# Folding the column transforms of a spectral block over f and -f: fewer products on TensorE, more sums on GpSimd and VectorE

## The chip, the core and the metric

The kernel runs on one core of a Trainium2 chip. The metric is the device time of one execution in microseconds (us). The engines are named as in the profile: PE (TensorE, matrix products; PEld is its weight loads), DVE (VectorE), ACT (ScalarE), POOL (GpSimd) and SP (SyncE, which here only issues DMAs). Each engine works through its own queue in order; queues wait for each other by semaphores.

## What is computed

The reference, cut to what matters (one batch, S = 2048 rows, D = 512 columns, F = 1376, all in float32):

```python
def _A_ref(x, w_r, w_i):                      # spectral filter
    X = rfft2(x, axes=(-2, -1))
    X = X * (w_r + 1j * w_i)
    return irfft2(X, s=(S, D), axes=(-2, -1))

def _B_ref(x, w1, b1, w2):                    # Dense -> Mish -> Dense
    h = x @ w1 + b1
    return (h * tanh(softplus(h))) @ w2

mod = (silu(c) @ w_mod).reshape(1, 6, 1, -1)
sa, ca, ga, sb, cb, gb = (mod[:, i] for i in range(6))
h = layernorm(x) * (1 + ca) + sa
x = x + ga * _A_ref(h, A_w_r, A_w_i)
h = layernorm(x) * (1 + cb) + sb
x = x + gb * _B_ref(h, B_w1, B_b1, B_w2)
```

## The kernel before

The transforms are products with constant matrices. The 2048 rows are seen as 128 x 16 (16 blocks n), the 512 columns as 128 x 4, and the half spectrum as 64 column frequencies q with 8 values each (4 lanes, real and imaginary). The order of each engine's instructions is that of the program, stage by stage, written by hand; tile pools with two buffers per tag ("g1", "g2", "t", "y", "h") and two PSUM banks per tag ("A" to "D") decide how far one step can run ahead of another.

**Stage one**, for each block n (the loop at L342): `p1_row` multiplies the transposed x by row constants that hold the scale 1 + ca (four full-precision products, L203). DVE takes the statistics of x (`norm_sums`, L117 and L118), ACT guesses the reciprocal deviation (`norm_guess`), DVE refines it (`norm_refine`, L130). `p1_mean` (L218) subtracts the mean's part, `p1_cast` and `p1_low` (L234, L241) split the result into a high and a low half in the reduced-precision type. `p1_split` does the same for the column constants of the block (ACT L195, POOL L196) and makes a negated copy (L197). `p1_col` then forms the complex column product with nine reduced-precision products (L248 to L250), and `p1_save` copies it to `a_sb`. The gate's and shift's sums that this stage needs are the `shift_sum` calls; `shift_rows` ends the stage.

**Stage two** works on 17 groups of column frequencies: fifteen of four, one of three, and one that holds the special frequencies (`z_...`). `seq` is their order, with the special group fifth. For each group: `p2_in` transposes `a_sb` on PE and copies it to a buffer z (ACT, L464), POOL adds the shift to one column per frequency (`p2_shift`, L472); `p2_mul` applies the 16-point part of the row transform (L482); `p2_prod` multiplies by the filter on DVE (L498) and adds and subtracts (L503, L504: both on POOL, the first on DVE for the first three and last two groups); `p2_back` transposes (L515) and copies (L518); `p2_out` applies the inverse (L528); `store_d` writes the result to `d` with two copies and two negated copies on ACT. The first eight `p2_in` come ahead of the loop (LEAD = 8); in step s of the loop stand `p2_prod` of group s, `p2_mul` of s + 1, `p2_in` of s + 3 (from s = 5), `mod_late`, `p2_back` of s - 2 and `p2_out` of s - 3. `mod_late` forms the gates and second shift and scale from `w_mod`, sixteen sums on DVE over the steps (L98, L100, L110); `mod_fetch` loads what they need.

**Stage three**, for each block n (the loop at L902): `p3_col` makes the inverse column transform with eight products (four with the constants `kc[0]`, L663, and four with `kc[1]`, L664), ACT copies, `p3_row` makes the inverse row transform (four products, L673) and DVE adds it to x (L676). Between them stand the second statistics (L117), the loads and splits of w1 (ACT L621, POOL L622) and w2 (L714, L715), and the first blocks' normalisation and transposition (L655).

**The MLP** runs 48 items with a lag of two items between its first and second product (`mlp`, L858).

## Time and profile before

| | |
|---|---|
| median of 3 runs | 392.95 us (391.5 to 393.79) |
| the profiled execution | 391.52 us, of which the span is 389.4 us |
| granted PE clock, mean | 1.0 |
| instructions | 7386 |
| stage one: first save to last save of the column product | about 16.3 to 50.1 us |
| stage two: first transposes to last store | about 50.2 to 98.9 us |
| stage three: first inverse product to first product of the MLP | 98.9 to 142.1 us |
| MLP | 142.1 to 389.4 us |

How to read the profile's lines: a group's line names the source line, the engine, the operation, output and inputs, the shape and the count; behind the bar stand its busy time in us and the mean of one in ns, then the idle time of the engine just ahead of it and what ended that. A line of the order of time starts with the start and the duration in us. One full-precision product is two MATMUL records; a reduced-precision one and a transposition are one record each. A matmul's end is modelled, so the distance between starts is what counts.

### The profile page before, as it was taken

How to read it: one execution, taken by the hardware profiler on the slowest of the kernel's cores; microseconds unless marked ns; L12 is line 12 of the kernel's file. 1: busy time of each engine (PE TensorE's matmuls, PEld its weight loads, DVE VectorE, ACT ScalarE, POOL GpSimd, SP SyncE). 2: the span in 40 equal slices, each digit the busy share in tenths (PEclk: the TensorE clock that was granted, in tenths of full speed). 3: DMA queues.
4: the chain of work that ended last, by engine and by line, in shares of the span. 5: the costliest groups of instructions: out<-in, count | busy, mean ns of one | idle time of the engine just before them, and what ended most of it. 6: DMA issues, size and time to landing. Idle time of an engine off the chain costs nothing.

```text
span 389.4 us, 7386 instructions
## 1 busy us (share of the span) xinstructions
PE 383.1 (98%) x2752; PEld 355.4 (91%) x2752; DVE 298.8 (77%) x668; ACT 247.9 (64%) x546; POOL 96.1 (25%) x132
## 2 busy tenths in 40 slices
PE   8999999999999999999999999999999999999996
PEld 8889889999999998999998998999999999899984
DVE  2888978876299989887856965965966875987993
ACT  1798756678559648975855765674674674594751
POOL 0687737665077533300000000000000010017000
PEclk9999999999999999999999999999999999999999
DMA  7999993472132411100100100100100200123011
GB/s 237 383 323 339 347 344 109 133 300 63 47 124 78 145 49 28 56 3 0 56 0 3 54 2 0 56 0 2 55 2 0 76 0 2 46 65 106 3 54 54
DMA packets 21027, 36.44 MB, mean 94 GB/s; under 512 B 3680, under 2 KB 6592, under 8 KB 20736
## 3 DMA queue, kind: packets, MB, share of 16 engines
q1 hardware_dynamic: 20992, 35.98, 27.1%
q8 instruction: 21, 0.34, 0.3%
q14 instruction: 14, 0.11, 0.1%
HBM read 31.78 MB, written 4.19 MB: 92 GB/s over the span
## 4 chain that ended last, share of the span: by engine, by line
PE 86%; DMA 4%; DVE 3%; ACT 3%; issue 1%; SPq 1%; POOL 1%; POOLq 0%; DVEq 0%
PE bank L805 24%; PE bank L752 20%; PE bank L754 10%; PE bank L482 3%; PE bank L528 3%; PE bank L673 3%; PE bank L663 3%; PE bank L664 3%; PE bank L797 2%; PE bank L248 2%; DMA x<-in_A_x_dram 2%; PE bank L203 2%; PE bank L817 2%; PE bank L642 2%; PE bank L461 2%; DMA mraw<-in_km_dram 2%
## 5 line engine op out<-in xcount | busy, mean ns | idle before, releaser
L762 ACT ACTIVATE buf<-bank,b1n 128x256 f32<-128x256 f32 (+1 forms) x88 | 40.8, 472 | 66.8 <-PE bank L754 66.4
L763 DVE TENSOR_TENSOR buf<-buf,bank 128x256 f32<-128x256 f32 (+1 forms) x88 | 35.4, 417 | 38.6 <-ACT buf L762 38.6
L715 DVE TENSOR_TENSOR al<-buf,ah 128x512 fp32r<-128x512 f32 (+2 forms) x85 | 53.5, 653 | 0.7 <-ACT ah L714 0.7
L734 POOL TENSOR_TENSOR buf<-buf,modr 128x512 f32<-128x512 f32 (+1 forms) x3 | 3.9, 1292 | 183.0 <-DMA buf<-in_B_w_dram 175.7
L752 PE MATMUL bank<-h2e,w1h 128*128 128x512 f32 (+1 forms) x176 | 48.4, 397 | 0.0
L752 PE MATMUL bank<-h2o,w1h 128*128 128x512 f32 (+1 forms) x176 | 48.3, 396 | 0.0
L714 ACT CAST ah<-buf 128x512 fp32r<-128x512 f32 (+2 forms) x85 | 43.0, 548 | 1.2 <-DVE buf L779 1.2
L779 DVE TENSOR_TENSOR buf<-buf 128x128 f32<-128x128 f32 x148 | 39.9, 311 | 3.5 <-ACT buf L769 2.2
L769 ACT ACTIVATE buf<-buf 128x512 f32<-128x512 f32 (+1 forms) x48 | 28.6, 596 | 14.8 <-DVE buf L763 14.7
L805 PE MATMUL bank<-w2a,ah 128*128 128x256 f32 x161 | 34.9, 286 | 0.0
L752 PEld LDWEIGHTS bank<-h2o,w1h 128*128 128x128 f32 (+1 forms) x176 | 30.2, 187 | 4.5
L752 PEld LDWEIGHTS bank<-h2e,w1h 128*128 128x128 f32 (+1 forms) x176 | 30.1, 187 | 4.5
L805 PE MATMUL bank<-w2b,ah 128*128 128x256 f32 x147 | 31.8, 283 | 0.0
L754 PEld LDWEIGHTS bank<-h2o,w1l 128*128 128x128 f32 (+1 forms) x176 | 26.7, 185 | 4.2
L754 PEld LDWEIGHTS bank<-h2e,w1l 128*128 128x128 f32 (+1 forms) x176 | 26.7, 185 | 4.2
L754 PE MATMUL bank<-h2e,w1l 128*128 128x256 f32 (+1 forms) x176 | 27.8, 280 | 0.0
L754 PE MATMUL bank<-h2o,w1l 128*128 128x256 f32 (+1 forms) x176 | 27.8, 280 | 0.0
L805 PEld LDWEIGHTS bank<-w2a,ah 128*128 128x128 f32 x161 | 26.7, 191 | 0.0
L663 PE MATMUL bank<-kc,d 128*128 128x128 f32 x128 | 24.7, 275 | 0.0
L664 PE MATMUL bank<-kc,d 128*128 128x128 f32 x128 | 24.7, 275 | 0.0
L805 PEld LDWEIGHTS bank<-w2b,ah 128*128 128x128 f32 x147 | 24.6, 191 | 0.0
L117 DVE BATCH_NORM_STATS2 st<-x 128x6 f32<-128x512 f32 x32 | 22.1, 689 | 0.8 <-DMA x<-in_A_x_dram 0.4
(227 smaller groups left out, 1002.7 us busy)
## 6 DMA issues: line engine op xcount, KB each, us to landing
buf<-in_B_w_dram SPq DMA_DIRECT2D x20, 256.0 KB, 2.8
x<-in_A_x_dram SPq DMA_DIRECT2D x16, 256.0 KB, 4.9
xring<-in_x_t_dram SPq DMA_DIRECT2D x16, 256.0 KB, 5.1
wm<-in_w_mod_dram SPq DMA_DIRECT2D x16, 256.0 KB, 4.2
out_dram<-x SPq DMA_DIRECT2D x7, 512.0 KB, 2.6
mraw<-in_km_dram SPq DMA_DIRECT2D x16, 128.0 KB, 5.0
wqa<-in_w_q_dram SPq DMA_DIRECT2D x8, 256.0 KB, 4.8
wqb<-in_w_q_dram SPq DMA_DIRECT2D x8, 256.0 KB, 5.5
```

The source lines that it names most:

```text
L117: nc.vector.bn_stats(t, x[:, n, :])
L663: nc.tensor.matmul(o, dj[:, 0:128], kc[0][:, n, :], start=True, stop=False)
L664: nc.tensor.matmul(o, dj[:, 64:192], kc[1][:, n, :], start=False, stop=True)
L714: nc.scalar.copy(h, r)
L715: nc.vector.tensor_tensor(l, r, plain(h), op=ALU.subtract)
L752: nc.tensor.matmul(ps, w1h[:, k, fs], h[:, k], start=(k == 0), stop=False)
L754: nc.tensor.matmul(ps[:, 0:256], w1l[:, k, fs], h[:, k, 0], start=False, stop=(k == 3))
L762: nc.scalar.activation(o, ps[:, 256:], AF.Identity, bias=b1n[:rows, f:f + 1])
L763: nc.vector.tensor_tensor(o, o, ps[:, 0:256], op=ALU.add)
L769: nc.scalar.activation(o, o, AF.Mish)
L779: nc.vector.tensor_tensor(o, p, q, op=op)
L805: nc.tensor.matmul(o, a[p][:, e], w2[t][q][:, r], start=(own and half == 0 and t == 1 and i == 0), stop=(end and i == 2 and (n, half) != ( ...
```

## The change

The column transform is folded over the frequencies f and -f. The constants of the first column product now are 128 real columns: cosines for 64 frequencies, sines for 63, and the alternating column of frequency 64; so one real full-precision product per block (`p1_col`) takes the place of nine reduced-precision ones, and splitting, casting and the low halves go. `p1_save` turns the sine half by -i with three ACT instructions. The mean's part is made apart: POOL forms row sums times mean (`p1_rank`), and DVE scales and adds in one instruction (`p1_norm`); the first two blocks keep `p1_mean` and are scaled on ACT. `first_scale` makes the negated mean times reciprocal deviation as well (`norm_shift`).

In stage two, f and -f are joined by a sum and a difference per group, on POOL for all groups (`fold(nc.gpsimd, ...)` in `p2_in`), and taken apart again with a sum and a difference on DVE from PSUM (`fold(nc.vector, ...)` in `p2_back`); the ACT copy of `p2_back` becomes half as wide. Groups now have 127 rows. Frequency 64 of all column groups is gathered by small POOL copies in `zh` and taken through a branch of its own (`half_mul`, `half_prod`, `half_back`, `half_out`) in the last steps; its result is put in the last row of `dd` by a DMA on SP's queue. `store_d` has three ACT instructions instead of four. The sums of `mod_late` are on DVE as before.

In stage three `p3_col` needs four products instead of eight, and `kc` and `km` are half as large. The loads of `km` bring two blocks each. The w2 buffers move to other tags.

The diff, cut to its core:

```diff
     def first_scale(lo, hi):
-        norm_refine(lo, hi, -1, st.pop(("r", lo)))
+        norm_refine(lo, hi, -1 if lo < 2 else 1, st.pop(("r", lo)))
+        if lo >= 2:
+            norm_shift(lo, hi)
...
     def load_m(n):
-        nc.sync.dma_start(mraw[:, n, :], km_d[:, n, :])
+        if n % 2 == 0:
+            nc.sync.dma_start(m[:, n:n + 2, :], km_d[:, n:n + 2, :])
...
+    def p1_scale(n):
+        st["g", n] = g = buf("g1")
+        nc.scalar.activation(g, st.pop(("pg", n)), AF.Copy, scale=rstd[:, n:n + 1])
+
+    def p1_rank(n):
+        st["km", n] = t = buf("g2")
+        nc.gpsimd.tensor_scalar(t, kb, nmr[:, n:n + 1], 0.0, op0=ALU.mult, op1=ALU.add)
+
+    def p1_norm(n):
+        st["g", n] = g = buf("g1")
+        nc.vector.scalar_tensor_tensor(g, st.pop(("pg", n)), rstd[:, n:n + 1], st.pop(("km", n)),
+                                       op0=ALU.mult, op1=ALU.add)
+
+    def p1_col(n):
+        st["pa", n] = pa = bank("C")
+        nc.tensor.matmul(pa, m[:, n, :], st.pop(("g", n)), start=True, stop=True)
 
     def p1_save(n):
-        nc.scalar.copy(a_sb[:, :, n, :], st.pop(("pa", n)).rearrange("p (e q) -> p q e", e=8))
+        pa = st.pop(("pa", n)).rearrange("p (e q) -> p q e", e=8)
+        nc.scalar.copy(a_sb[0:H, :, n, :], pa[0:H])
+        nc.scalar.copy(a_sb[H:P, :, n, 0:4], pa[H:P, :, 4:8])
+        nc.scalar.mul(a_sb[H:P, :, n, 4:8], pa[H:P, :, 0:4], -1.0)
...
+            p1_col(n)
+            if n % 2 and n + 2 < N2:
+                first_scale(n + 1, n + 3)
+                p1_rank(n + 1)
+                p1_rank(n + 2)
             if n + 3 < N2:
-                p1_split(n + 3)
                 norm_sums(n + 3)
                 if n % 2 == 0:
                     first_guess(n + 2, n + 4)
+            if 1 <= n and n + 1 < N2:
+                p1_norm(n + 1)
...
+        nc.scalar.copy(dd[0:H, :, :, qs], src[0:H])
+        nc.scalar.mul(dd[H:end, :, 0, qs], src[H:end, :, 1, :], -1.0)
+        nc.scalar.copy(dd[H:end, :, 1, qs], src[H:end, :, 0, :])
...
+    def fold(eng, z, far):
+        eng.tensor_tensor(z[..., H:U], z[..., 1:H], far, op=ALU.subtract)
+        eng.tensor_tensor(z[..., 1:H], z[..., 1:H], far, op=ALU.add)
 
     def z_in():
...
+        nc.gpsimd.memset(z[:, 0:3 * P], 0.0)
...
     def z_back():
...
+        nc.gpsimd.memset(t1[:, 0:3 * P], 0.0)
         nc.gpsimd.memset(t2[0:96, 0:P], 0.0)
...
+    def half_prod():
+        pb = st.pop(("pb", "h"))[0:NQ, 0:P].rearrange("p (c j) -> p c j", c=2)
...
+    def half_out():
+        pd = bank("D")
+        nc.tensor.matmul(pd[:, 0:NQ], kv[:, 512:640], st.pop(("t", "h"))[:, 0:NQ], start=True, stop=True)
+        nc.scalar.copy(zh, pd[:, 0:NQ])
+        nc.sync.dma_start(dd[U:P].rearrange("p a c q -> p (a c) q")[:, :, 1:NQ], zh[:, 1:NQ])
 
     def p2_in(g):
...
-        nc.scalar.copy(z[:, 0:w], ps[:, 0:w])
-        st["z", g] = z
+        st["z", g] = zbuf(g)
+        z = turned(g)
+        src = ps[:, 0:nq * P].rearrange("p (q b s) -> p q b s", q=nq, b=2)
+        nc.scalar.copy(z.rearrange("p q (b s) -> p q b s", s=H)[:, :, 0:3:2, :], src)
+        fold(nc.gpsimd, z, z[:, :, P:P + U - H])
+        nc.gpsimd.tensor_copy(zh[:, q0:q0 + nq], z[:, :, 191])
...
     def p2_back(g):
...
         t = buf("t")
-        nc.scalar.copy(t[:, 0:w], pc[:, 0:w])
+        tv, src = (v[:, 0:w].rearrange("p (q s) -> p q s", s=P) for v in (t, pc))
+        nc.scalar.copy(tv[:, :, 0:H], src[:, :, 0:H])
+        fold(nc.vector, tv, src[:, :, H:U])
...
+            for i, fn in enumerate((half_mul, half_prod, half_back, half_out)):
+                if s == len(seq) - 3 + i:
+                    fn()
...
     def p3_col(n):
-        d = dd[n // 8][:, n % 8]
         pe = bank("A")
         for j in range(4):
-            dj = d[:, j].rearrange("p c q -> p (c q)")
-            o = pe[:, j * P:(j + 1) * P]
-            nc.tensor.matmul(o, dj[:, 0:128], kc[0][:, n, :], start=True, stop=False)
-            nc.tensor.matmul(o, dj[:, 64:192], kc[1][:, n, :], start=False, stop=True)
+            nc.tensor.matmul(pe[:, j * P:(j + 1) * P], dd[:, 4 * n + j].rearrange("p c q -> p (c q)"), kc[:, n, :],
+                             start=True, stop=True)
```

(H = 64, U = 127, P = 128.)

More of the change, by code (lines that the diff above doesn't have):

```diff
@@ L141, in norm_scale @@
         norm_refine(lo, hi, 1)
[L142 to L143 removed]
+        norm_shift(lo, hi)
     def norm_stats(ns):
@@ L237, in p1_low @@
-    def p1_low(n):
-        c = st.pop(("c", n))
-        if n not in POOL_LOW:
-            gh, gl = st["g", n]
-            nc.vector.scalar_tensor_tensor(gl, c, rstd[:, n:n + 1], plain(gh), op0=ALU.mult, op1=ALU.subtract)
-    def p1_col(n, part=range(3)):
-        m = mt(n)
-        gh, gl = st["g", n]
-        pa = bank("C") if part[0] == 0 else st["pa", n]
-        for i, (a, g) in list(enumerate(((0, gh), (1, gh), (0, gl))))[part[0]:part[-1] + 1]:
-            nc.tensor.matmul(pa, m[:, a, 0:128], g, start=(i == 0), stop=False)
-            nc.tensor.matmul(pa[:, 0:256], m[:, a, 256:384], g[:, 256:512], start=False, stop=False)
-            nc.tensor.matmul(pa[:, 256:512], m[:, a, 128:256], g[:, 0:256], start=False, stop=(i == 2))
-        st["pa", n] = pa
+    def p1_scale(n):
+        st["g", n] = g = buf("g1")
+        nc.scalar.activation(g, st.pop(("pg", n)), AF.Copy, scale=rstd[:, n:n + 1])
@@ L415, in z_mul @@
         pb = bank("B")
-        reflected(pb[:, 0:160], z, lambda i: kf[:, 128 + 160 * i:288 + 160 * i])
+        for i in range(3):
+            nc.tensor.matmul(pb[:, 0:160], z[:, i * P:(i + 1) * P], kf[:, 128 + 160 * i:288 + 160 * i],
+                             start=(i == 0), stop=(i == 2))
         st["pb", 0] = pb
@@ L1044, in bwd @@
         return matrix((n, 16), fn).transpose(2, 0, 1, 3, 4, 5).reshape(32 * n, 128)
-    zero = [bwd(5, unlanes(r)) for r in (None, 15 - k2, (16 - k2) % 16)]
-    kv = np.concatenate([bwd(4, backward)] + [m[:128] for m in zero], 1)
+    turn = np.conj(half)
+    near, far = bwd(5, unlanes(None)), bwd(5, unlanes((16 - k2) % 16))
+    zero = [near + far, near - far,
+            bwd(5, lambda v: -1j * turn * (unlanes(None)(v) + unlanes(15 - k2)(v)))]
+    kv = np.concatenate([bwd(4, backward)] + [m[:128] for m in zero] + [bwd(4, lambda v: turn * backward(v))], 1)
     kw = np.concatenate([m[128:] for m in zero], 0)
-    out = dict(kr=kr.reshape(128, 4, 128), km=km.reshape(128, 16, 256), kc=kc,
+    out = dict(kr=kr.reshape(128, 4, 128), km=km, kc=kc,
                ki=ki.reshape(128, 4, 128), kf=kf, kv=kv, kw=kw, kp=np.eye(128))
@@ L1058, in _layout @@
     p, k, q = np.arange(128), np.arange(16), np.arange(64)
-    own = p[:, None] + 128 * k
-    far = (128 - p[:, None] + 128 * k) % 2048
+    f = np.concatenate([p[:64], -p[1:64], [64]])[:, None]
+    own = (f + 128 * k) % 2048
+    far = (128 - f + 128 * k) % 2048
     def pick(row, col):
```

217 lines of the change are left out of this document (99 added, 118 removed).

## The prediction, made before the run

> **What bounds the kernel now.** I read the page first (busy shares, the slices, the chain), then a table of the four stages, then each engine's order of time inside the stages.
>
> ```profile
> PE 383.1 (98%) x2752; PEld 355.4 (91%) x2752; DVE 298.8 (77%) x668; ACT 247.9 (64%) x546; POOL 96.1 (25%) x132
> PEclk9999999999999999999999999999999999999999
> PE 86%; DMA 4%; DVE 3%; ACT 3%; issue 1%; SPq 1%; POOL 1%; POOLq 0%; DVEq 0%
> ```
>
> By the page PE sets the time: 98% busy, 86% of the chain that ended last. The stages tell more. Each row below is a stretch, its length, then busy time of PE, PEld, DVE, ACT, POOL, the granted clock, DMA share and GB/s: stage one (row and column products), stage two (per-column-group transforms), stage three (inverse products, first weights), then the MLP.
>
> ```profile
> 14.40:50.20 35.80, 35.14 (x249) 31.91 (x248) 31.27 (x80) 28.99 (x65) 25.64 (x36) 1.00 1.02 344
> 50.20:98.90 48.70, 47.87 (x401) 45.24 (x401) 36.77 (x71) 33.81 (x104) 28.15 (x50) 1.00 0.53 186
> 98.90:142.10 43.20, 43.05 (x385) 42.85 (x384) 36.21 (x67) 27.47 (x57) 23.36 (x24) 1.00 0.30 91
> 142.10:389.40 247.30, 243.65 (x1632) 222.60 (x1630) 187.93 (x428) 152.45 (x310) 16.47 (x15) 1.00 0.08 28
> ```
>
> PE leads everywhere, but DVE follows at 31.3 of 35.8, 36.8 of 48.7 and 36.2 of 43.2 us. A cut of PE's work in stages one and three is therefore worth only the distance to DVE. In stage two DVE has 11.9 us free and POOL 20.5, and that is where the change puts new work. The MLP is not touched.
>
> **Stage one.** The nine reduced-precision products per block and the split of the constants go. One full-precision 128x512 product comes.
>
> ```profile
> 42.22 0.49 PE L248 MATMUL bank<-buf,mring 128*128 128x512 f32 x1
> ...
> 43.72 1.05 PE L203 MATMUL bank<-modr,xring 128*128 128x128 f32 x8
> 44.52 0.48 PE L248 MATMUL bank<-buf,mring 128*128 128x512 f32 x1
> ...
> 98.05 1.02 PE L558 MATMUL bank<-modr,ones 128*128 128x512 f32 x2
> 98.92 0.27 PE L663 MATMUL bank<-kc,d 128*128 128x128 f32 x1
> ```
>
> Start to start, the column products take 43.72 - 42.22 = 1.50 us and the row products 0.80, so 2.30 per block. The same shape in full precision is the gate's sum L558: 98.05 to 98.92, 0.87 us. PE falls to 1.67 per block. DVE does not fall as far:
>
> ```profile
> 23.59 0.74 DVE L241 SCALAR_TENSOR_TENSOR buf<-bank,rstd,buf 128x512 fp32r<-128x512 f32 x1
> 24.25 0.68 DVE L117 BATCH_NORM_STATS2 st<-x 128x6 f32<-128x512 f32 x1
> 24.96 0.18 DVE L118 BATCH_NORM_AGGREGATE mv<-st 128x2 f32<-128x6 f32 x1
> 25.06 0.72 DVE L218 SCALAR_TENSOR_TENSOR bank<-modr,mv,bank 128x512 f32<-128x512 f32 x1
> 25.80 0.16 DVE L130 SCALAR_TENSOR_TENSOR ve<-mv,bank 128x2 f32<-128x2 f32 x1
> ...
> 26.25 0.69 DVE L117 BATCH_NORM_STATS2 st<-x 128x6 f32<-128x512 f32 x1
> ...
> 45.28 0.69 DVE L110 SCALAR_TENSOR_TENSOR bank<-wms,modr 128x512 f32<-128x512 f32 x1
> ```
>
> Statistics cost 0.81 (24.25 to 25.06). The new normalising operation has the shape and PSUM input of L241 and L218, 0.66 to 0.74; I take 0.70. Refinement takes 0.45 per pair of blocks (25.80 to 26.25), the added shift another 0.15. A pair is 1.62 + 1.40 + 0.60 = 3.6, plus a wait, since the normalising operation now needs POOL's product of the row sums with the mean; bounds 0 to 0.9, and 0.3 taken, as other DVE work stands between. That is 1.95 per block against PE's 1.67. From about 14.3 (the third statistics, 0.66 earlier because the first L241 goes): 13 statistics 10.5, 14 normalisings 9.8, 7 refinements 4.2, 3 shift sums 2.0, 7 waits 2.1, together 28.6. The last normalising ends near 43; product and save add 2.5, since the save is three ACT instructions in place of one. Stage two then starts near 45.6: **4.5 us earlier**. Bounds: 2 us (more DVE waits) to 8 us (PE's 0.63 x 13). DMA carried 344 GB/s at full share; a block's transfers shrink from 640 to 576 KB, 1.67 us at that rate, so they follow. ACT loses the casts, POOL the splits: neither is late.
>
> **Stage two, POOL.** Each of 16 groups gets two folds on POOL (128 x 4x63; one group 3x63), a small copy, and there are two memsets.
>
> ```profile
> L504 POOL TENSOR_TENSOR buf<-buf 128x256 f32<-128x256 f32 x15 | 13.1, 872 | 2.5 <-DVE buf L498 1.7 <-PE bank L515 0.8
> L503 POOL TENSOR_TENSOR buf<-buf 128x256 f32<-128x256 f32 x11 | 8.8, 800 | 9.4 <-PE bank L515 3.8 <-PE bank L403 2.1 <-POOL buf L472 1.3
> L197 POOL TENSOR_SCALAR mring<-mring 128x256 fp32r<-128x256 f32 x16 | 6.8, 427 | 1.4
> ```
>
> A fold is L503's operation with 252 elements in place of 256. Its bounds are 0.43 (L197, one input) and 0.87 (L504 mean). I take 0.73 to 0.75, as below, because it is the same operation with two inputs in SBUF. The strides (four runs of 63) are not in this trace.
>
> ```profile
> 51.33 0.20 POOL L472 TENSOR_TENSOR early<-early,saz 128x3 f32<-128x3 f32 x1 [4.27 <-ACT early L464]
> ...
> 65.59 1.18 POOL L504 TENSOR_TENSOR buf<-buf 128x256 f32<-128x256 f32 x1
> 66.73 0.65 POOL L472 TENSOR_TENSOR buf<-buf,saz 128x4 f32<-128x4 f32 x1
> ...
> 68.02 0.73 POOL L504 TENSOR_TENSOR buf<-buf 128x256 f32<-128x256 f32 x1
> 68.70 0.21 POOL L472 TENSOR_TENSOR buf<-buf,saz 128x4 f32<-128x4 f32 x1
> ...
> 68.87 0.21 POOL L442 MEMSET buf<- 96x128 f32 x1
> ...
> 93.67 0.95 POOL L504 TENSOR_TENSOR buf<-buf 128x256 f32<-128x256 f32 x1 [0.78 <-DVE buf L498]
> ```
>
> ```profile
> 65.20 0.98 DVE L100 SCALAR_TENSOR_TENSOR modr<-wm,sc,modr 128x512 f32<-128x512 f32 x1
> 66.10 1.21 DVE L110 SCALAR_TENSOR_TENSOR wm<-wm,modr 128x512 f32<-128x512 f32 x1
> ```
>
> POOL's sum: 28.2 now, + 30 x 0.75 + 2 x 0.6 for folds = 23.7, + 16 copies at 0.15 (the pace behind L472) = 2.4, + memsets of 384 columns at up to 0.5 each = 0.9. Then collisions: L504 needs 1.18 while the gates' sums L100 and L110 run, and 0.73 without, so 0.45 per gate sum. Sixteen make 7.2; the rows now hold about 4.5 of it (15 x 0.14 + 11 x 0.07 + the slow L472), so + 2.7. **POOL has 58 us of work in stage two.** It can start 1.1 us in (51.33, when the first group is copied) and behind its last sum stand today 94.6 to 98.9, 4.3 us. Without one wait, stage two is 63.4 us instead of 48.7. POOL's in-order queue makes it so: the folds of the eight leading groups (some 14 us) stand ahead of the second group's product sums, and PE, ACT and DVE wait for those.
>
> [...]
>
> **Stage two, DVE and the waits.**
>
> ```profile
> L763 DVE TENSOR_TENSOR buf<-buf,bank 128x256 f32<-128x256 f32 x80 | 32.1, 417 | 31.7 <-ACT buf L762 31.7
> L498 DVE TENSOR_TENSOR buf<-bank,wqb 128x512 f32<-128x512 f32 x16 | 10.2, 680 | 0.6 <-POOL buf L504 0.6
> 71.18 1.01 POOL L503 TENSOR_TENSOR buf<-buf 128x256 f32<-128x256 f32 x1 [2.09 <-PE bank L403]
> ```
>
> DVE's own folds read PSUM as L763 does: 32 x 0.42 = 13.4. With the half-frequency branch (four small ones, under 0.4 each) and the zero group, 36.8 becomes about 51.5, also over 48.7, but under POOL: a step has two L498, one gate sum and two folds, 1.3 + 0.7 + 0.8 = 2.8, against POOL's 1.4 + 1.5 + 0.3 + 0.45 = 3.65. PE (2.7 by its 401 records) and ACT (five copies instead of six, as many elements) stay below.
>
> Waits that POOL cannot fill: (a) after the leading folds, DVE's products wait for POOL to free their two buffers, then POOL for them: 0 to 3, 1.8 taken. (b) At the zero group POOL now clears a tile that ACT, then DVE, must write before the next product: today's wait is 2.09 (71.18), so 2 to 3; 2.6 taken, of which none is in the sum. (c) At the end, DVE has about 9 us queued behind the last group's folds (three products, the branch, four folds), more than POOL's three sums: 1 to 8, 2.6 taken, the nearest to the DVE sum alone. The branch's last row goes by DMA on SP's queue behind two weight loads which wait for the last transposes.
>
> ```profile
> buf<-in_B_w_dram SPq DMA_DIRECT2D x20, 256.0 KB, 2.8
> ```
>
> At 2.8 it lands about when the last group is stored; 0 to 3 late, nothing taken. Sum of waits 7.0; **stage two 70.4 us, 21.7 longer**.
>
> **Stage three.** Four of twelve products per block go: 64 x 2 records at 43.2 / 385 = 0.112, 14.3 us of PE. But DVE:
>
> ```profile
> 103.58 0.69 DVE L676 TENSOR_TENSOR x<-x,bank 128x512 f32<-128x512 f32 x1 [8.42 <-PE bank L673]
> ...
> 106.26 0.69 DVE L676 TENSOR_TENSOR x<-x,bank 128x512 f32<-128x512 f32 x1 [1.05 <-PE bank L673]
> ...
> 144.66 0.69 DVE L676 TENSOR_TENSOR x<-x,bank 128x512 f32<-128x512 f32 x1 [0.64 <-PE bank L673]
> ```
>
> After 106.26 DVE waits for PE only once more, 0.64. It gains the earlier first addition (4.7 us behind the stage's start, now about 3.1), the 1.05 and the 0.64: **3.3 us**; bounds 1 and 7. The other 11 us of PE's saving become idle time before the first gated items.
>
> **Sum.** -4.5 + 21.7 - 3.3 = +13.9. The profiled execution took 391.5 (span 389.4, 2.1 around it), at the low end of the runs (median 392.95), so 405.4 against it and 1.4 more against the median. I say 405.5; own range 399 to 412.
>
> **Rivals.** *POOL without waits:* its sum alone, 63.4; then +6.9, 398.5 (395 to 399). For it: POOL runs up to five sums back to back today; against it: (a) and (b) follow from two buffers. *A cheap fold, the other side:* if a fold costs 0.43 as L197, POOL's sum falls by 10 and DVE's 51.5 plus a 2.5 tail decides: stage two 54, net -2.5, 389. The change stops being slower where stage two is under 56.5, a fold under about 0.53 with no waits; L503's rows speak against it. *PE alone decides,* as the page's 98% reads: -0.63 x 16 - 14.3, 367; DVE's rows speak against it. *PE's clock falls:* PE would now wait in stage two, for several us in the leading part; the PEclk row shows 9 throughout, so no drop was seen. At half rate a step's 2.7 becomes 5.4, 1.75 over POOL's, for nine steps: 421.
>
> [...]
>
> **Chances.** Forecast 0.61; POOL without waits 0.14; cheap fold 0.11; PE alone 0.02; clock 0.06; gains and losses that cancel (390 to 394) 0.06. The range 391 to 414 leaves out the cheap fold, PE alone and the clock, 0.19. A measurement of this kernel can tell 0.5% from nothing: faster by more 0.13, within 0.06, slower 0.81.
>
> **What would show it.** Right: POOL busy over 55 us in stage two with hardly a gap between its steps; PE and ACT waiting there for POOL's sums; stage two near 70 us; DVE without idle time in stage three while PE waits; the first transposes near 45.6. Wrong: folds under 0.53 us, stage two under 57 us, or stage three shorter by over 7.

## The result and the profile after

The changed kernel takes 415.56 us (median of 4 runs, 414.76 to 415.64) against 392.23 (391.29 to 393.79): 1.059 times as long, interval 1.054 to 1.063. The direction and the stage were forecast; the time lies 10 us above the forecast (405.5) and 1.6 above the wider of its two ranges (391 to 414). The profiled execution took 415.61 us, its span 413.8.

The page of the changed kernel: busy shares, the granted PE clock in 40 slices, and the chain of work that ended last.

```profile
PE 377.0 (91%) x2517; PEld 337.7 (82%) x2517; DVE 307.8 (74%) x703; ACT 242.4 (59%) x533; POOL 103.6 (25%) x156
PEclk9989989989968999999999999999999999999999
PE 61%; DVE 9%; POOL 5%; ACT 3%; issue 2%; POOLq 0%; DVEq 0%; ACTq 0%
```

PE lost 235 instructions but only 6 us of busy time, its share of the chain fell from 86% to 61%, and its clock is no longer full throughout (0.97 on average in place of 1.00). The stages of the same execution (stretch, length, busy time of PE, PEld, DVE, ACT, POOL, granted clock, DMA share, GB/s); the last row is the end of stage two alone:

```profile
16.30:49.00 32.70, 28.17 (x137) 18.83 (x136) 27.38 (x80) 22.46 (x63) 9.52 (x14) 0.95 1.01 345
49.00:126.30 77.30, 58.87 (x404) 52.15 (x405) 50.90 (x107) 36.37 (x97) 53.76 (x98) 0.89 0.33 104
126.30:165.50 39.20, 31.79 (x257) 30.53 (x256) 33.76 (x64) 26.02 (x54) 23.57 (x24) 0.96 0.32 93
165.50:413.80 248.30, 243.64 (x1632) 222.82 (x1630) 189.48 (x431) 152.88 (x312) 16.47 (x15) 1.00 0.08 29
109.00:126.30 17.30, 13.95 (x71) 11.44 (x72) 7.82 (x19) 8.34 (x23) 3.26 (x4) 0.70 0.23 64
```

| us | before | after | difference | forecast |
|---|---|---|---|---|
| to the first scaling of the row constants | 7.6 | 9.6 | +2.0 | 0 |
| stage one from there | 42.6 | 39.4 | -3.2 | -4.5 |
| stage two | 48.7 | 77.3 | +28.6 | +21.7 |
| stage three | 43.2 | 39.2 | -4.0 | -3.3 |
| MLP | 247.3 | 248.3 | +1.0 | 0 |

The differences add up to the spans' 24.4. Stage two holds the loss and most of the miss. POOL's steady step there, in order of time, with DVE's gate sums (L113):

```profile
95.68 0.81 DVE L113 SCALAR_TENSOR_TENSOR wm<-wm,modr 128x512 f32<-128x512 f32 x1
95.90 1.17 POOL L374 TENSOR_TENSOR early<-early 128x252 f32<-128x252 f32 x1
97.15 0.72 POOL L375 TENSOR_TENSOR early<-early 128x252 f32<-128x252 f32 x1
...
98.10 0.74 POOL L521 TENSOR_TENSOR buf<-buf 127x256 f32<-127x256 f32 x1
98.79 0.74 POOL L522 TENSOR_TENSOR buf<-buf 127x256 f32<-127x256 f32 x1
99.16 0.92 DVE L113 SCALAR_TENSOR_TENSOR wm<-wm,modr 128x512 f32<-128x512 f32 x1
99.48 1.18 POOL L374 TENSOR_TENSOR early<-early 128x252 f32<-128x252 f32 x1
```

A fold takes 0.72 us, or 1.17 beside a gate sum, and a step 99.48 - 95.90 = 3.58: the forecast had 0.73 to 0.75, 0.45 more beside a gate sum, and 3.65. Each of the two longer folds ends 0.58 us after the gate sum that ran when it started (97.07 behind 96.49, 100.66 behind 100.08), and so do the other nine full-size folds and sums of this stage that started during one, within 0.02 us. The end of the stage, in order of time on all engines:

```profile
108.80 0.20 POOL L490 TENSOR_TENSOR early<-early,saz 128x4 f32<-128x4 f32 x1
...
111.43 0.43 DVE L521 TENSOR_TENSOR buf<-buf 127x256 f32<-127x256 f32 x1 [1.78 <-PE bank L533]
...
114.96 0.94 POOL L522 TENSOR_TENSOR buf<-buf 127x256 f32<-127x256 f32 x1 [2.52 <-DVE buf L516]
115.24 1.21 DVE L103 SCALAR_TENSOR_TENSOR modr<-wm,sc,modr 128x512 f32<-128x512 f32 x1
...
116.81 0.42 DVE L375 TENSOR_TENSOR buf<-buf,bank 128x252 f32<-128x252 f32 x1
...
117.38 2.05 PE L548 MATMUL bank<-kv,buf 128*127 128x128 f32 x8 [0.83 <-DVE buf L375]
...
119.50 0.37 ACT L537 COPY buf<-bank 128x256 f32<-128x256 f32 x1 [3.99 <-PE bank L548]
...
121.05 3.78 PE L548 MATMUL bank<-kv,buf 128*127 128x128 f32 x16 [0.46 <-ACT dd L356]
...
126.32 1.95 PE L682 MATMUL bank<-kc,dd 128*128 128x128 f32 x16
```

From POOL's last work on a group's input (109.00) to stage three (126.32) pass 17.3 us. Before, that work (L472) ended at 89.53 and stage three began at 98.92, 9.4 us later:

```profile
88.84 0.69 POOL L472 TENSOR_TENSOR buf<-buf,saz 128x4 f32<-128x4 f32 x1
```

This stretch is called **the end** below. The reader is to see the sequence: DVE works without a gap from 111.43 to 117.23 and only then lets PE on to the next group's last products; PE then needs 2.05 us for eight L548 that take 1.12 at full clock (below); and ACT's copy waits 3.99 us for those.

### The profile page after: what moved, and what is told of

The parts are those of the page before. It is cut to its first block, busy times and chain, and to the rows that moved or that the text cites. A ratio compares the mean times of both kernels' runs of the same rounds, so it can differ in the third digit from the quotient of the medians.

```text
span 413.8 us, 6957 instructions
## 1 busy us (share of the span) xinstructions
PE 377.0 (91%) x2517; PEld 337.7 (82%) x2517; DVE 307.8 (74%) x703; ACT 242.4 (59%) x533; POOL 103.6 (25%) x156
## 4 chain that ended last, share of the span: by engine, by line
PE 61%; DVE 9%; POOL 5%; ACT 3%; issue 2%; POOLq 0%; DVEq 0%; ACTq 0%
PE bank L822 23%; PE bank L769 19%; PE bank L771 9%; PE bank L814 2%; PE bank L834 2%; DVE st L120 2%; DVE x L695 2%; PE bank L664 2%; PE bank L548 1%; POOL early L374 1%; POOL buf L521 1%; POOL buf L522 1%; POOL early L375 1%; PE bank L692 1%; DVE buf L516 1%
## 5 line engine op out<-in xcount | busy, mean ns | idle before, releaser
L780 DVE TENSOR_TENSOR buf<-buf,bank 128x256 f32<-128x256 f32 (+1 forms) x88 | 35.3, 416 | 38.6 <-ACT buf L779 38.6
L769 PE MATMUL bank<-h2o,w1h 128*128 128x512 f32 (+1 forms) x176 | 48.3, 396 | 0.0
L786 ACT ACTIVATE buf<-buf 128x512 f32<-128x512 f32 (+1 forms) x48 | 28.6, 596 | 14.8 <-DVE buf L780 14.7
L822 PE MATMUL bank<-w2c,ah 128*128 128x256 f32 x196 | 35.8, 283 | 0.0
L822 PEld LDWEIGHTS bank<-w2c,ah 128*128 128x128 f32 x196 | 30.5, 192 | 0.0
L822 PE MATMUL bank<-w2c,al 128*128 128x256 f32 x98 | 27.8, 283 | 0.0
L500 PE MATMUL bank<-kf,early 128*127 128x128 f32 x126 | 18.8, 298 | 7.8 <-POOL early L490 7.3
L500 PEld LDWEIGHTS bank<-kf,early 128*127 128x127 f32 x126 | 16.8, 208 | 10.6 <-POOL early L490 8.7
L692 PE MATMUL bank<-kiv,buf 128*128 128x128 f32 x128 | 18.6, 291 | 7.4 <-ACT buf L685 4.7
L692 PEld LDWEIGHTS bank<-kiv,buf 128*128 128x128 f32 x128 | 16.4, 200 | 8.7 <-ACT buf L685 5.6
```

The costliest lines, as they stand in the source:

```text
L500: nc.tensor.matmul(pb[0:U, 0:w].rearrange("p (e q) -> p e q", q=nq)[:, :, i], z[:, i, 0:U], kf[:, 0:128], start=True, stop=True)
L692: nc.tensor.matmul(px[:, j * P:(j + 1) * P], e[:, j * P:(j + 1) * P], kiv[:, j, :], start=True, stop=True)
L769: nc.tensor.matmul(ps, w1h[:, k, fs], h[:, k], start=(k == 0), stop=False)
L780: nc.vector.tensor_tensor(o, o, ps[:, 0:256], op=ALU.add)
L786: nc.scalar.activation(o, o, AF.Mish)
L822: nc.tensor.matmul(o, a[p][:, e], w2[t][q][:, r], start=(own and half == 0 and t == 1 and i == 0), stop=(end and i == 2 and (n, half) != ( ...
```

## The experiments

Fifteen kernels were run, all derived from the changed one. Stage two runs from the first transposes to the first inverse product, by each kernel's own profile; the part before the end is the difference of the two columns. Both columns are of one execution each. Within one kernel the executions differ by up to 6 us: a fall of PE's clock in stage one, which comes in some executions only, costs about 1.2 us each time, and the first scaling stands 7.9 to 9.6 us behind the start.

| run | median us | ratio to before, interval | stage two | the end | clock in stage two |
|---|---|---|---|---|---|
| before | 391.4 to 392.3 | | 48.7 | 9.4 | 1.00 |
| after | 415.56 | 1.054 to 1.063 | 77.3 | 17.3 | 0.89 |
| e1_half_tile | 413.9 | 1.052 to 1.060 | 77.2 | 16.4 | 0.89 |
| e2_zero_early | 410.7 | 1.042 to 1.054 | 73.5 | 17.3 | 0.91 |
| e3_fold_pe | 404.7 | 1.027 to 1.042 | 67.4 | 19.1 | 0.95 |
| e4_warm_tail | 417.8 | 1.063 to 1.069 | 80.5 | 20.0 | 0.92 |
| e5_lead_dve | 414.5 | 1.050 to 1.061 | 75.0 | 15.1 | 0.95 |
| e6_half_apart | 411.8 | 1.049 to 1.054 | 75.6 | 15.7 | 0.91 |
| e7_spread | 399.9 | 1.019 to 1.023 | 62.4 | 14.4 | 1.00 |
| e8_lead5 | 411.8 | 1.044 to 1.054 | 75.1 | 17.3 | 0.91 |
| e9_no_fold | 402.9 | 1.024 to 1.029 | 64.6 | 18.7 | 0.97 |
| e10_warm | 413.4 | 1.050 to 1.056 | 76.0 | 16.1 | 1.00 |
| e11_out_pe | 420.4 | 1.068 to 1.075 | 82.4 | 17.9 | 0.94 |
| e12_best | 399.4 | 1.015 to 1.020 | 62.4 | 14.4 | 1.00 |
| e13_no_out | 408.1 | 1.040 to 1.045 | 72.9 | 12.2 | 0.93 |
| e14_no_folds | 392.7 | 0.999 to 1.003 | 55.2 | 12.9 | 1.00 |
| e15_waits | 405.95 | 1.035 to 1.039 | 69.8 | 13.3 | 1.00 |

### The waits, one by one

The first theory was that POOL's order of work sets stage two and that the waits on top were undersized; its rivals were that PE's clock, or DVE, sets it.

**e1_half_tile**: the branch's turned tile from an idle ring.

```diff
-        st["t", "h"] = t = buf("t")
+        st["t", "h"] = t = buf("h")
```

> Edit: the half-frequency branch takes its turned tile from a ring that is idle in stage two, in place of the ring t of the column groups. In the trace of the changed kernel the copy of the group before the last (L537) waited 3.99 us for the products L548, and the folds behind it waited 2.68 us on DVE, because the branch had taken one of the two t tiles. If that ring sets the end of stage two, the run gives 2.7 us less than 415.6, about 412.9. Rival: behind it stand the two PSUM banks of the last products, of which the branch holds one, and PE at a lower clock (L548 x8 in 2.05 us in place of 1.05), so that the last products cannot start earlier; then at most 0.5 us less, 415.1 to 415.6.

Stage two did not move (77.2; the end 0.9 us shorter, the part before it 0.8 longer), as the rival said. The folds that had waited now stood 8.2 us behind the end's beginning in place of 10.9, but the last products still waited for the bank, and the stage's granted clock was 0.89 again. So the first theory was wrong about this wait. The median of 413.9 lies between the two expectations; the four executions took 412.7 to 415.0, and the profiled one 414.9.

**e2_zero_early**: the zero group's two tiles from the idle ring, cleared before the first fold.

```diff
+        st["t0"] = t1, t2 = buf("h"), buf("h")
+        nc.gpsimd.memset(t1[:, 0:3 * P], 0.0)
+        nc.gpsimd.memset(t2[0:96, 0:P], 0.0)
         for i in range(8):
...
-        t1, t2 = buf("t"), buf("t")
+        t1, t2 = st.pop("t0")
```

> Edit: the two tiles that the zero group clears on POOL before its second transform come from an idle ring and are cleared before stage two's first fold. In the trace of the changed kernel ACT waited 5.2 us for the clearing (L419), DVE 4.2 us behind ACT, and POOL then 3.40 us for DVE's product L516. If this wait is a delay of the whole stage, it goes: 3.4 us and the 0.6 us of the clearing itself, so 411.6 (411 to 412.5). Rival: POOL's queue is late anyway and another wait takes the place, then less than 1 us, 414.6 or more.

Stage two fell by 3.8 us, all of it ahead of the end, about the 4.0 expected. These are the rows of the changed kernel that show the wait (order of time):

```profile
79.07 0.42 POOL L419 MEMSET buf<- 128x384 f32 x1
...
79.52 0.21 ACT L421 COPY buf<-bank 128x64 f32<-128x64 f32 x1 [5.22 <-POOL buf L419]
80.00 0.22 DVE L424 TENSOR_TENSOR buf<-buf,bank 128x63 f32<-128x63 f32 x1 [4.18 <-POOL buf L420]
...
83.02 1.04 POOL L521 TENSOR_TENSOR buf<-buf 127x256 f32<-127x256 f32 x1 [3.40 <-DVE buf L516]
```

A clearing of 0.42 us costs 3.8, because it stands behind a group's sums and folds in POOL's queue, while ACT, DVE and at last POOL itself wait for it in a ring.

**e6_half_apart**: the whole branch apart from the groups' rings and banks.

```diff
-        st["pb", "h"] = pb = bank("B")
+        st["pb", "h"] = pb = bank("A")
...
-            t = buf(("g1", "g2")[i])
+            t = h[:, i * P:(i + 1) * P]
...
-        st["y", "h"] = y = buf("y")[0:NQ]
+        st["y", "h"] = y = h[0:NQ, 2 * P:3 * P]
...
-        pc = bank("C")
+        pc = bank("A")
...
-        pd = bank("D")
+        pd = bank("A")
```

> Edit: the whole half-frequency branch goes through tiles of an idle ring and the PSUM bank of the finished first transposes, in place of the rings of the column groups (products, sums, turned tiles, banks B, C and D); its instructions stay where they are in each queue. Moving its turned tile alone gave nothing in stage two (77.2 us against 77.3). If the branch's banks are the next in the row (the last products waited for a bank that the branch held: L500 0.47 and 0.9 us, L548 0.46 to 0.86 us), the end comes 2 to 4 us earlier: stage two 73.5 to 75.5, 411.5 to 413.5. Rival: DVE's own queue there (products, branch, gate sum and folds back to back for 5.8 us) and PE at half clock set the end, then at most 1 us less: 414.6 to 415.6.

The end took 15.7 us, 1.6 less, still with the halved clock. The median is the one expected, stage two lies between the two expectations. The clock was at half for 6.8 us of this end and for 10.2 of the changed kernel's, so part of the 1.6 may be the clock's.

**e5_lead_dve** and **e8_lead5**: less folding on POOL ahead of the first products, and fewer groups ahead of the loop.

```diff
-        fold(nc.gpsimd, z, z[:, :, P:P + U - H])
+        fold(nc.vector if seq.index(g) in (1, 3, 5, 7) else nc.gpsimd, z, z[:, :, P:P + U - H])
```

> Edit: of the leading groups' folds in stage two, every second one (four groups, eight folds) goes from POOL to DVE, which stood idle there for 3.7, 0.9, 2.7 and 2.0 us while it waited for the first products. If POOL's queue sets stage two, it loses 8 x 0.72 = 5.8 us of work: 415.6 - 5.8, about 410 (409 to 411.5). Rival: two engines that fold side by side get in each other's way, as POOL's folds took 1.17 to 1.23 us beside the gates' sums in place of 0.72; then some 0.45 us of each of POOL's eight remaining leading folds are lost, 413 to 414. Second rival: POOL's queue is not what sets the end, and nothing is gained, 415 to 416.

POOL lost 3.9 us of work in the stage (49.86 busy against 53.76), and the part before the end still took 59.9 us, as after. POOL now stood idle for DVE's products instead, and the zero group's wait took what was left. That contradicts the expectation: here work taken from POOL ahead of the zero group gave nothing. What this run did give is a price of the clock, below.

```diff
-LEAD = 8
+LEAD = 5
```

> Edit: five column groups in place of eight are transposed and folded ahead of the loop; the other three come inside it, one step each. No work is added or taken away. If POOL's amount of work sets stage two, the order changes only the wait after the leading folds (about 1 us of idle time on POOL): 414 to 416. Rival: the eight leading folds in front of the first sums are the delay (DVE idle 9 us in all until 65.8 us), and DVE and PE start earlier: 5 us less, about 410.5.

2.2 us less ahead of the end, between the two.

### PE's clock

The run e5_lead_dve kept the clock in the end, with the end's instructions unchanged. Its order of time, and below it the row by stretch:

```profile
106.06 0.20 POOL L490 TENSOR_TENSOR early<-early,saz 128x4 f32<-128x4 f32 x1
...
114.65 1.12 PE L548 MATMUL bank<-kv,buf 128*127 128x128 f32 x8 [1.01 <-DVE buf L375]
...
121.35 0.82 PE L682 MATMUL bank<-kc,dd 128*128 128x128 f32 x5 [0.46 <-ACT dd L356]
```

```profile
106.26:121.30 15.04, 10.27 (x71) 8.32 (x71) 7.82 (x19) 8.35 (x23) 3.28 (x4) 1.00 0.23 74
```

The same 71 PE records fill 10.27 us in place of 13.95, and the end takes 15.1 us in place of 17.3. **The halved clock costs 2.2 us there**, by one execution of each. It was the fastest of e5_lead_dve's four, 410.3; the others took 414.0 to 415.2 at a lower mean clock (0.97 to 0.98 in place of 0.99).

**e4_warm_tail** and **e10_warm** tried to hold the clock with products that nobody reads.

```diff
         pc = bank("C")
+        for i in range(4 if seq.index(g) >= 13 else 0):
+            nc.tensor.matmul(pc[:, 0:P], ones, ones, start=True, stop=True)
```

> Edit: in the last four steps of stage two PE gets products that nobody reads (four before each group of transposes and four before each group of last products, written to the bank that the next ones overwrite), so that it does not stand idle. In the trace of the changed kernel the granted clock was 0.70 from 110 to 125 us, and eight L548 took 2.05 us there in place of 1.05. If the falling clock is what lengthens the end, the clock stays near 1.0 there and the run gives 2.5 to 3.1 us less, about 412.5 to 413.1. Rival: the end is set by DVE's queue and by tiles, and the added products only delay PE: 415.6 to 417.5.

The stage's clock was 0.92 in place of 0.89, but the end took 20.0 us: the added products stood in front of transposes for which DVE's sums waited. This run does not tell what the clock is worth. e10_warm put such products where PE waits anyway (here the stage one part):

```diff
         st["pa", n] = pa = bank("C")
+        for _ in range(5 if n == 2 else 0):
+            nc.tensor.matmul(pa[:, 0:P], ones, ones, start=True, stop=True)
```

> Edit: the changed kernel with products that nobody reads, placed on PE only where it waits anyway: five in the gap of 1.9 us in stage one, three behind each leading group, eight in the wait for the zero group, some in the last four steps. In four of nine executions with the same stage one the clock stayed at 1.00 there and the stage took 38.2 to 38.3 us; in the other five it fell to 0.66 to 0.75 for 5 us and the stage took 39.4 to 40.6. In the end of stage two the same instructions took 15.1 us at 1.00 and 17.3 at half clock. If the clock falls because PE waits, it stays near 1.0 in every execution: 415.6 - 1.2 - 2.2 and up to 1 us more in the leading part, 411 to 412.5, and the runs spread less. Rival: the fall has nothing to do with the waiting, or the added products delay as much as the clock gives: 415 to 417.

The clock stayed at 1.00 through stage two; the median fell by 2.2 us to 413.4 (412.0 to 414.2), about half of what was expected, and the runs spread no less. In stage one the clock no longer fell behind the gap that was filled (1.00 from 14 to 28 us), but the stage still took 39.5 us, about as long as with one fall. Ahead of the end stage two took 59.9 us, as in the changed kernel: there the full clock gave nothing. In the end it took 16.1, 1.2 less. So with PE's waits filled the clock did not fall in stage two (1.00 in place of 0.89); the last section shows how busy PE was ahead of the falls of the changed kernel.

### Whose folds

**e3_fold_pe**: the folds before the products made by PE, with a matrix of 1 and -1 in place of the identity.

```diff
-            nc.tensor.transpose(ps[:, i * P:(i + 1) * P],
-                                a_sb[:, q0 + i, :, :].rearrange("p n e -> p (n e)"), ident)
+            nc.tensor.matmul(ps[:, i * P:(i + 1) * P],
+                             a_sb[:, q0 + i, :, :].rearrange("p n e -> p (n e)"), kg, start=True, stop=True)
...
-        fold(nc.gpsimd, z, z[:, :, P:P + U - H])
```

> Edit: the fold of f and -f before the products is made by PE, as the transposing product with a matrix of 1 and -1 in place of the identity, for all 16 groups; the 32 folds leave POOL. PE gets one more record of about 0.12 us for each of 63 columns, 7.5 us. If POOL's work sets stage two (53.8 us busy of 77.3, of which the folds are some 23), it falls to PE's 48.6 + 7.5 = 56 us and the queue at the end, some 60 to 64 in all, and the run gives 398 to 402. If PE sets it (its busy time in the stage is 58.9), the run is slower by up to 7.5: 416 to 423. If DVE with its own folds (50.9 busy) sets it, 400 to 404 with DVE busy all through.

Stage two fell by 9.9 us to 67.4 and the run to 404.7, less than expected: the part before the end came to 48.3, with PE and DVE both nearly full in the steady steps, but the end took 19.1. Rows by stretch: the stage, some steady steps, and most of the end:

```profile
46.20:113.60 67.40, 60.01 (x467) 55.85 (x467) 49.03 (x107) 36.53 (x97) 29.97 (x66) 0.95 0.39 124
76.00:86.00 10.00, 10.00 (x91) 9.97 (x90) 9.90 (x23) 6.38 (x16) 6.88 (x15) 1.00 0.65 219
96.00:113.60 17.60, 12.71 (x71) 10.43 (x69) 9.03 (x21) 9.18 (x25) 3.04 (x4) 0.81 0.21 62
```

**e9_no_fold**: those folds left out on every engine.

```diff
-        fold(nc.gpsimd, z, z[:, :, P:P + U - H])
```

> Edit: the fold before the products is left out (no engine makes it, so the columns of f and -f are used as they are); the plain transposes, the products, DVE's folds behind them and all the rest stay. It is the rival of the prediction in which a fold costs nothing. By that rival DVE's 51 us and a short end decide: stage two 54, 389 to 392. By the runs so far the end of stage two (17.6 us from the last group's copy to stage three, with the folds on PE) stays whatever POOL does, and the steps before it go at DVE's 2.9 us: stage two 61 to 64, 397 to 401, still slower than before.

402.9 us, and 64.6 in stage two, a little more than expected: with that fold for nothing the change still loses 10.6 us. The cheap-fold rival (389) is refuted in its price, not only in its condition.

**e11_out_pe**: DVE's folds moved to PE's second transposing product.

```diff
-            nc.tensor.transpose(pc[:, i * P:i * P + U], y[:, 0:w].rearrange("p (e q) -> p e q", q=nq)[:, :, i],
-                                ident[0:U, 0:U])
+            nc.tensor.matmul(pc[:, i * P:(i + 1) * P], y[:, 0:w].rearrange("p (e q) -> p e q", q=nq)[:, :, i],
+                             ko[0:U], start=True, stop=True)
...
-        fold(nc.vector, tv, src[:, :, H:U])
```

> Edit: the folds behind the products, which the change put on DVE (32 of 0.42 us, 13 us in all), are made by PE's second transposing product with a matrix of 1 and -1; POOL keeps its folds. If POOL's 3.6 us sets the steady steps, they do not change and only the end gets shorter by the folds that stand in DVE's queue there (2 to 3 us): 412 to 414. Rival: DVE is the bound of stage two behind POOL's back (50.9 us busy of 77.3), and the run gives 405 or less. If PE's added 7.5 us count, 418 to 423.

420.4 us. PE became the bound: eight records of L535 took 1.86 us from start to start, twice what eight of L548 or L502 take, and its steps took 4.07 us (97.44 to 101.51):

```profile
97.44 0.60 PE L478 MATMUL bank<-ident,a_sb 128*128 128x128 f32 x4
97.88 2.03 PE L535 MATMUL bank<-ko,buf 127*128 127x128 f32 x8
99.74 1.05 PE L548 MATMUL bank<-kv,buf 128*127 128x128 f32 x8
100.63 1.05 PE L502 MATMUL bank<-kf,early 128*127 128x128 f32 x8
101.51 0.60 PE L478 MATMUL bank<-ident,a_sb 128*128 128x128 f32 x4
```

It says nothing of DVE's share. That came from leaving DVE's folds out:

**e13_no_out** and **e14_no_folds**.

```diff
-        nc.scalar.copy(tv[:, :, 0:H], src[:, :, 0:H])
-        fold(nc.vector, tv, src[:, :, H:U])
+        nc.scalar.copy(tv[:, :, 0:U], src[:, :, 0:U])
```

> Edit: the folds behind the products are left out on DVE (the turned tile is copied as it is); POOL's folds and all the rest stay. If POOL sets the steady steps (3.6 us each), these do not change, and only the end, where DVE's queue holds up the last products, gets shorter by 2 to 4 us: stage two 73 to 75, 411.5 to 413.5. Rival: DVE's folds are part of the bound all along, as with POOL's folds gone stage two still took 64.6 us: then 65 to 70 and 402 to 408.

```profile
46.70:119.60 72.90, 55.60 (x404) 49.97 (x404) 39.12 (x75) 39.93 (x98) 53.46 (x98) 0.93 0.33 113
107.41:119.60 12.19, 9.52 (x71) 8.10 (x71) 3.92 (x9) 9.79 (x26) 3.27 (x4) 1.00 0.31 91
```

Ahead of the end nothing changed (60.7 us against 60.0): there POOL sets the time, and DVE's folds are covered, as predicted. In the end they are not: 12.2 us against the 15.1 of e5_lead_dve at the same full clock, 2.9 us. The median, 408.1, lies below the 411.5 to 413.5 expected and at the rival's edge. Of the 7.1 us between the two profiled executions stage two gives 4.4, as the first expectation has it; an earlier first scaling gives 1.5 and stage one, here at full clock, 0.8, and both vary without this edit.

> Edit: all folds are left out, those on POOL and those on DVE; the half-frequency branch and the new zero group stay. With POOL's folds alone left out stage two took 64.6 us. If DVE's folds are the rest of the difference to before's 48.7, it takes 50 to 53 now, 388 to 391. If the branch, the zero group's wait and the end are, it stays at 57 to 62, 395 to 400.

55.2 us and 392.7 in all, between the two expectations and with no difference from before that could be measured. So without any fold 22.1 of the 28.6 us go, the lower clock among them (1.00 here); left out singly the two kinds of folds gave 12.7 and 4.4. The other 6.5 us, of which 3.5 are in the end, use up what stages one and three save. Which part of the change they come from was not tried apart.

### Do the waits add up?

**e15_waits**: every fold where the change put it, but the zero group cleared early, the branch apart, the last gate sums one or two steps earlier, and the unread products of e10 (without those for the zero group).

```diff
-    when = (3, 4, 5, 6, 6, 7, 8, 9, 9, 10, 11, 12, 12, 13, 14, 16)
+    when = (3, 4, 5, 6, 6, 7, 8, 9, 9, 10, 11, 12, 12, 13, 13, 14)
```

> Edit: the changed kernel with every fold where the change put it, but the zero group's tiles cleared early, the half-frequency branch apart, the last two gates' sums one and two steps earlier, and unread products on PE in stage one's gap, behind the leading groups and in the last steps. If the single savings add up (3.8 for the zero group, 1.6 for the branch, 2.2 for the clock in the end, 1.2 for the gate sum), stage two takes 77.3 - 8.8 = 68.5 us, near the prediction's 70.4, and the run gives 405 to 408. Rival: they overlap, as POOL's work alone is 54 us and the next wait takes the place: stage two 72 to 74, 409.5 to 412.

```profile
47.50:117.30 69.80, 58.90 (x475) 54.41 (x475) 51.51 (x108) 36.47 (x98) 53.72 (x96) 1.00 0.36 116
103.95:117.30 13.35, 12.75 (x100) 11.33 (x100) 6.68 (x18) 8.51 (x24) 3.28 (x4) 1.00 0.28 82
```

69.8 us in stage two and 405.95 in all (405.4 to 406.3): 7.5 of the expected 8.8 us. With POOL's work unchanged (53.7 us) these waits are worth as much as the whole miss in stage two, 6.9. The end became 4.0 us shorter, the part before it 3.5. e10_warm had the same unread products in its end and the same full clock, and its end took 16.1: the 2.8 us between the two are the branch's place and the last gate sums together, as the 1.6 of e6_half_apart and the 1.2 expected of the gate sum would have it.

### A better version

**e7_spread** shares the fold between PE (nine groups) and POOL, with five leading groups, the zero group cleared early, the branch apart and all gate sums one to three steps earlier; **e12_best** also puts the last group's second transposes ahead of the last products but two and fills the gap in stage one.

```diff
+    def on_pe(g):
+        return seq.index(g) in (0, 1, 2, 3, 6, 9, 12, 15, 16)
```

> Edit, several together: the fold before the products is made by PE's transposing product for nine of the groups (the first four, every third one then, and the last two) and stays on POOL for the others; five groups lead in place of eight; the zero group's tiles are cleared early; the half-frequency branch is apart, as in the run before; the gates' sums come one or two steps earlier. PE then has 48.6 + 9 x 0.47 = 53 us of work in stage two, DVE 51, POOL about 41. If it is the sum of work on the busiest engine that counts, stage two takes 56 to 59 us, and the run gives 395 to 398. Rival: the 17.6 us that the end took with all folds on PE as well (from the last group's copy to the first product of stage three) stay: stage two 62 to 65, 400 to 404.

```diff
-            if 2 <= s < len(seq) + 2:
+            if 2 <= s < len(seq) + 1:
                 p2_back(seq[s - 2])
+            if s == len(seq):
+                p2_back(seq[s - 1])
```

> Edit: the spread version (folds shared by PE and POOL, five leading groups, the branch apart, the tiles cleared early, the gates' sums earlier; 399.9) with two more: the last group's second transposes stand ahead of the last products but two on PE, and the unread products fill the gap in stage one. By the order in time of its end (last products waiting 1.25 us for DVE, the copy of the last group 1.3 us late on ACT) 1 to 1.5 us less, and up to 1 us less in stage one: 397.5 to 399. Against the kernel before it stays slower: PE's extra fold products, 4.2 us, and an end 4 us longer than before's 9.4 outweigh what stages one and three gain. Rival: the end is at what ACT needs for its last three stores and nothing is gained: 399.5 to 400.5.

399.9 and 399.4 us: 16 us better than the change, and still 2.1 and 1.8% slower than before. With 62.4 us in stage two the first came out as its rival said, and the second gave next to nothing, again as its rival said: stage two 62.4 and the end 14.4 in both.

## Why the prediction was wrong in size, point by point

- **What bounds the kernel**: right. DVE kept stages one and three from gaining PE's saving, and POOL became the bound of stage two's steady part.
- **Stage one, 4.5 us**: right where the clock held. In six executions of this code with the clock at 1.00 behind its gap of 1.9 us the stage took 38.3 to 38.6 us from the first scaling, 4.0 to 4.4 less than before's 42.6. In seven others PE's clock fell behind that gap (0.86 between 16 and 28 us; 0.50 for 3.41 us in the changed kernel's trace); three of them took 39.4, the profiled one among them, and four 40.6. In two of these four, e2_zero_early and e8_lead5, the clock was also 0.74 and 0.64 between 43 and 46 us. The stage also began 2.0 us later, behind the last load of the scale's weights; in the other runs the first scaling stood between 7.9 and 9.4. Why it varies was not tried. (A block's transfers are 1.71 us at the rate named, not 1.67, as a KB is 1024 bytes; DVE's 1.95 covers either.)
- **POOL's work, 58 us**: the size of a fold was right (0.72, and 0.45 more beside a gate sum), the sum was 4.2 too high (53.8).
- **Waits (a) and (b), 1.8 and 2.6**: too low. POOL stood idle for 12.0 us between its first fold at 50.16 and the end of its last sum at 115.90 (65.7 less 53.8 busy), 3.6 of them in the end and 8.4 before; forecast for that part were 4.4. The zero group's wait alone is 3.8.
- **Wait (c), the end, is the step that failed.** Behind POOL's work the prediction put 2.6 us of waits and 4.3 us as before, 6.9 together; it took the value "nearest to the DVE sum alone" from a range of 1 to 8. Measured were 3.6 us of POOL's idle time (1.1 and 2.5) and 10.4 from its last sum at 115.90 to stage three: 14.0, so 7.1 more. The errors of the POOL sum (4.2 too high) and of the earlier waits (4.0 too low) cancel by luck, so this is the miss of 6.9 in stage two. The runs split it roughly: 2.2 PE's halved clock (e5), up to 1.6 the branch's place in the groups' rings and banks (e6), 2.9 DVE's folds (e13); the last gate sum's share was only tried together with others, in e15. DVE's queue itself had been listed (9 us), but it was set against POOL's three sums, although PE's last products and ACT's stores come behind it one after the other.
- **The branch's DMA, nothing taken**: right; it landed at 125.3, ahead of the last store at 126.1.
- **Stage three, 3.3 us**: right, 4.0, with the clock at half for 3.4 us in it. In the waits of that stage DVE stood idle mainly before its first addition, and PE waited for ACT's copies and for DVE:

```profile
DVE x L695 <- PE bank L692: 7.2, 3, 6.9
PEld bank L692 <- ACT buf L685: 5.6, 5, 2.9
PE bank L692 <- DVE x L695: 2.8, 2, 1.6
```

- **The rivals**: PE alone, POOL without waits and the cheap fold fell. The clock rival (0.06) was priced as a half rate through nine steady steps, which did not happen: from 85.3 to 116.0 us the clock was 1.00, and POOL hid PE. It did fall where PE waits most: in stage one, once in the leading part (54.6 to 58.0), at the zero group, in the end and in stage three. It counted in stage one and in the end, 1.2 and 2.2 us; ahead of the end it did not, as e10 shows. The half rate was the author's assumption, as no row of before shows a fall; the changed kernel's trace shows 0.50, but elsewhere than in those steps.

## What to carry to other kernels

When work moves to an engine with free time, add up that engine's queue, but work out the end of the stage by itself: there no next step covers anything, and an operation added to a group's path can stand in full. A small side branch is better kept out of the rings and banks of the main loop (up to 1.6 us here), and a buffer that must be cleared is better cleared where its engine is idle (3.8 us here). Idle time on a PE that had just been relieved came back here as a lower clock (0.97 in place of 1.00), so look at the granted clock by stretch before PE's saved time is counted as gained; in the changed kernel each of the four stretches of 3.41 us with PE busy for 30 to 44% had half clock behind it.

## What the runs showed of the hardware

**The clock fell after short gaps, but not after all of them.** In stage one all thirteen profiled executions of this code had the same PE gap, 1.79 to 2.01 us. After it, the changed kernel's PE ran at half pace, that of e5_lead_dve did not:

```profile
20.34 1.92 PE L234 MATMUL bank<-buf,m 128*128 128x512 f32 x2 [1.91 <-ACT a_sb L240]
22.05 1.92 PE L202 MATMUL bank<-modr,xring 128*128 128x128 f32 x8
```

```profile
18.80 1.10 PE L234 MATMUL bank<-buf,m 128*128 128x512 f32 x2 [1.90 <-ACT a_sb L240]
19.73 1.05 PE L202 MATMUL bank<-modr,xring 128*128 128x128 f32 x8
```

Behind that gap the clock fell in seven of the thirteen (0.86 between 16 and 28 us) and stayed at 1.00 in six. The changed kernel's trace shows five falls to 0.50 up to 150 us: four last 3.41 us and one, in the end, 10.24, three times as long, and they start at 20.48, 54.61, 81.92, 116.05 and 143.35, whole multiples of 3.41 us apart. So the clock of that execution can be read in stretches of 3.41 us on one grid. Two of them, and then two of e5_lead_dve, follow. The place of e5's grid is an estimate: its eight L476 at 55.26 take 1.51 us from start to start, in place of 0.88 at its earlier pace (four in 0.44 at 50.27), so a fall starts near 55.5, eleven times 3.41 behind 18.02.

```profile
17.07:20.48 3.41, 1.50 (x11) 1.09 (x10) 2.59 (x9) 2.79 (x8) 1.36 (x2) 1.00 1.05 390
20.48:23.89 3.41, 3.41 (x11) 2.38 (x12) 3.17 (x10) 1.65 (x5) 1.31 (x2) 0.50 1.03 361
```

```profile
14.61:18.02 3.41, 2.28 (x15) 1.61 (x13) 2.53 (x11) 2.35 (x7) 0.80 (x2) 1.00 1.05 369
18.02:21.43 3.41, 2.63 (x12) 1.76 (x13) 3.25 (x9) 2.31 (x8) 1.01 (x2) 1.00 1.06 386
```

In the changed kernel the gap lies in one stretch, PE is busy for 1.50 us of it (44%), and the next stretch is at 0.50. In e5_lead_dve the estimated grid cuts the gap in two, PE is busy for 67 and 77% of the two stretches, and the clock stays at 1.00. Between 10.2 and 143.4 us the changed kernel's trace holds 33 such stretches at full clock. In four PE was busy for 30 to 44% (those from 17.07, 51.20, 78.50 and 139.94), and half clock followed each time; of three with 52 to 55% one was followed by it (112.63), and of 26 with 61% or more none.

**A product that loaded an operand with a step took twice as long.** In e11_out_pe eight records of L535, which load y with a step of four elements, took 97.88 to 99.74, 1.86 us, while eight of L548, from a dense tile, took 0.89; their weight loads took 1.94 and 0.98. The plain transposes of the same y in the changed kernel (L533) did not pay it: four took 0.48 us, 110.75 to 111.23. The cause was not tried apart.
